# A fused attention and FFN kernel on one core: batch 0's scores as float32 products, and one decode form for all weight pieces

## The chip, the cores and the metric

The kernel runs on one core of one Trainium2 chip. The metric is the device time of one execution in microseconds (us). Three runs of the kernel before gave 784.2, 790.73 and 792.31 us; their median, 790.73 us, is the time before.

## What is computed

The reference is windowed attention followed by a two-layer FFN with a rational activation, in float32 (cut to what matters):

```
batch, n_heads, seq, head_dim = 4, 8, 768, 64      n_global, n_local = 8, 96
scores = (q @ k.T) / sqrt(D)
keep   = (key < n_global) | (0 <= rel < n_local)   # rel = query - key
scores += -2**-(h+1) * dist                        # head h's slope
a = softmax(where(keep, scores, -1e9));  o = a @ v # per head
x = o, heads side by side                          # (3072, 512)
h = x @ w_in                                       # w_in 512 x 2048
g = (a0 + a1 h + a2 h^2 + a3 h^3) / (1 + |b0||h| + |b1| h^2 + 1e-6)
out = g @ w_out                                    # w_out 2048 x 512
```

q, k, v and out are float32. The weights arrive as 64-bit numbers; the kernel reads each as two 32-bit words (`raw[:, :, 1]` and `raw[:, :, 0]`, `top` and `low` in `decode`) and builds a float32 number from them.

## The kernel before

**Units, chunks and steps.** Tokens are taken in 12 chunks of 256 (two tiles of 128). Attention is done in units: one unit `u` is one tile of 128 queries and one pair of heads, so there are 8 units in a chunk, 96 in all, and the first 24 units (`RAWQ = 24`) are batch 0. The FFN is done in items `f`, 8 for each chunk, each of 256 hidden columns. The main loop in `windowed()` runs over steps `t`; at step t it emits the load of unit t+4, the split of unit t+1, `st_qkT` and `st_qkE` of unit t, score and softmax of unit t-2, the transposes of unit t-3, the product with v of t-5, and FFN item f = t - 12 (`LAG`). So chunk 0's FFN items are steps 12 to 19.

**Order.** Each emitted piece carries a priority (1000 per step plus the table `PRI`, or `PRI_A` for the steps of the first FFN items). A planner that simulates the engines' time puts the instructions in order by these; on the chip each engine works its list in that order. Dependences are kept by semaphores. All DMAs are issued from SyncE's queue (SP), in one order as well.

**PSUM.** Four pools; the one that attention uses (`ps_t`, tag "t") has three buffers, shared by the transposed q and k (`tk`), the scores (`s`), the transposed probabilities (`tp`) and the attention output (`o`).

**Batch 0's scores.** For u < 24, `st_split` makes two float32r numbers out of each number of q and k: VectorE copies the rounded high part (line 377), GpSimd subtracts to get the low part (line 378). `st_qkT` transposes both parts of q and of k: 4 TensorE transposes (line 394). `st_qkE` brings them to SBUF on ScalarE: q with a scale for each head (line 412, twice), k (line 415) and, for a batch's first tile, the 8 global keys (line 417). High and low part of a head lie on the two halves of the 128 partitions, and two DMAs of 64 KB write the swapped copy of q that the second product needs (lines 413 and 414). `st_score` then takes 4 float32r products of 128 x 256 for each unit (line 450). From unit 24 on the split is done behind the transposes, by `raw_qkE` (lines 429 to 436), after a DMA within SBUF (line 372).

**Weight pieces.** `w_in` and `w_out` are decoded in 32 pieces of 128 x 512, in the order that `WSCHED` gives: 2 pieces at step 0, 4 at step 2, 6 each at 10 and 11, 4 at 12, 2 each at 13, 14 and 15, 4 at 18. Each piece is a load of 512 KB into one of three buffers (line 164, tile `r`), and then `decode` by one of four modes, listed in `MODE`:

- mode 0 (17 pieces): one ScalarE operation (line 172) and four VectorE operations: a maximum as a guard (174), a shift and mask (175), and two combinations of two tensors (177, 179);
- mode 1 (4 pieces): the same with the guard on GpSimd;
- mode 2 (9 pieces): one ScalarE operation (186), a conversion of 16 bits of the low word, here called the floor, on GpSimd (188), and two VectorE combinations (191, 193);
- mode 3 (2 pieces): the same with the floor on ScalarE (190).

**FFN.** Chunk 0's FFN uses the decoded float32 pieces as they are (lines 251 and 330). From chunk 1 on each product is made of three float32r products, of high and low parts (lines 259 and 335); for this `split_w` takes every piece apart at steps 15 to 26 (lines 210 and 211). Between the two products of an item stand `st_ew1` to `st_ew4` on ScalarE, VectorE and GpSimd (lines 283 to 315).

Of the kernel before, what the change touches and what calls it, by code (L numbers as in the profile page):

```python
# [17 lines left out]
P = 128  # L18
G = 8
# [5 lines left out]
RAW = 30  # L25
RAWQ = 24
LAG = 12
F2 = 2


# [4 lines left out]

SPLITS = {3: 0, 4: 1, 5: 6, 6: 7, 7: 10, 8: 19, 9: 20, 10: 25, 11: 26, 12: 28, 13: 29, 14: 32}

MODE = (3, 0, 2, 0, 2, 1, 2, 0, 0, 0, 0, 0, 0, 2, 2, 1, 0, 0, 0, 0, 0, 0, 0, 0, 2, 2, 1, 0, 3, 2, 1, 2)
HI_V = (2, 3, 6, 8, 11, 12, 13, 15, 16, 17, 18, 20, 21, 27, 28, 30, 31)
LO_V = (0, 2, 4, 5, 7, 8, 10, 13, 16, 17, 18, 20, 21, 22, 23, 24, 25)  # L40

# [55 lines left out]
def tile_kernel(ctx: ExitStack, tc: tile.TileContext, q, k, v, n_global, n_local,  # L97
# [24 lines left out]
    def unit(u):  # L122
        c, j = divmod(u, UPC)
        t, p = divmod(j, NPAIR)
        b, i = divmod(2 * c + t, NT)
        return c, t, p, b, i
# [32 lines left out]
    def decode(src, key):  # L159
        dst = full[key] = piece(F32, key)  # L160
        name = "r" + "_".join(map(str, key))
        raw = pl.ffn.tile([P, 2, 2, TOK], F32, tag="g", name=name, bufs=pl.gbufs)
        raw = raw.rearrange("p z a b -> p (z a b)").rearrange("p (f w) -> p f w", w=2)
        nc.sync.dma_start(out=raw.bitcast(I32), in_=src.rearrange("p (f w) -> p f w", w=2))
        bits = dst.bitcast(I32)
        top, low = raw.bitcast(I32)[:, :, 1], raw.bitcast(I32)[:, :, 0]
        half = raw.bitcast(U16).rearrange("p f (w z) -> p f w z", z=2)[:, :, 0, 1]
        mode = MODE[len(full) - 1]
        if mode < 2:


            nc.scalar.activation(out=dst, in_=raw[:, :, 1], func=AF.Abs)
            guard = nc.gpsimd if mode else nc.vector
            guard.tensor_scalar(out=dst, in0=dst, scalar1=1.125 * 2.0 ** -15, scalar2=None, op0=ALU.max)
            nc.vector.tensor_scalar(out=bits, in0=bits, scalar1=3, scalar2=0x3FFFFFFF,
                                    op0=ALU.logical_shift_left, op1=ALU.bitwise_and)
            nc.vector.scalar_tensor_tensor(out=bits, in0=top, scalar=-0x40000000, in1=bits,
                                           op0=ALU.bitwise_and, op1=ALU.bitwise_or)
            nc.vector.scalar_tensor_tensor(out=bits, in0=low, scalar=29, in1=bits,
                                           op0=ALU.logical_shift_right, op1=ALU.bitwise_or)  # L180
            return

        nc.scalar.activation(out=dst, in_=raw[:, :, 1], func=AF.Abs, scale=2.0 ** -112)
        if mode == 2:
            nc.gpsimd.tensor_scalar(out=low, in0=half, scalar1=2.0 ** -13, scalar2=FLOOR, op0=ALU.mult, op1=ALU.add)
        else:
            nc.scalar.activation(out=low, in_=half, func=AF.Copy, scale=2.0 ** -13, bias=FLOOR)  # L190
        nc.vector.scalar_tensor_tensor(out=low, in0=top, scalar=-0x80000000, in1=low,
                                       op0=ALU.bitwise_and, op1=ALU.bitwise_or)
        nc.vector.scalar_tensor_tensor(out=bits, in0=bits, scalar=3, in1=low,
                                       op0=ALU.logical_shift_left, op1=ALU.bitwise_or)
# [31 lines left out]
    def load_coef():  # L226
        nc.sync.dma_start(out=coef[:, 0:4], in_=ca.partition_broadcast(P))
        nc.sync.dma_start(out=coef[:, 4:6], in_=cb.partition_broadcast(P))
        nc.vector.memset(q1, 1.0 + 1e-6)
        nc.vector.memset(stats, 1e-9)  # L230

        rt = const.tile([P, 8], F32, name="rt")
        m, y, z, k = (rt[:, x:x + 1] for x in range(4))
        nc.scalar.activation(out=m, in_=coef[:, 5:6], func=AF.Abs)
        nc.vector.tensor_scalar(out=y, in0=m, scalar1=1e-36, scalar2=None, op0=ALU.max)
        nc.scalar.activation(out=y, in_=y, func=AF.Ln)
        nc.scalar.activation(out=y, in_=y, func=AF.Exp, scale=0.5)
        nc.vector.reciprocal(out=z, in_=y)
        nc.vector.scalar_tensor_tensor(out=z, in0=z, scalar=m, in1=y, op0=ALU.mult, op1=ALU.add)
        nc.vector.tensor_scalar(out=k, in0=m, scalar1=0.0, scalar2=0.5, op0=ALU.is_gt, op1=ALU.mult)  # L240
        nc.vector.tensor_tensor(out=b1, in0=z, in1=k, op=ALU.mult)
# [107 lines left out]

    kT = const.tile([P, H, 2, P], FR, name="kT")  # L350
    kG = const.tile([P, H, G], FR, name="kG")
    ident = const.tile([P, P], F32, name="ident")
    ident_r = const.tile([P, P], FR, name="ident_r")
    mask0 = const.tile([P, P], F32, name="mask0")
# [8 lines left out]
    def blocks_of(x, i):  # L363
        return x if i else x[..., 0, :]

    def st_split(u):
        p = unit(u)[2]
        if u >= RAWQ:

            if u % 2 == 0:  # L370
                s = pl.att.tile([P, 2, 4, D], FR, tag="rawq", name=f"sp{u}", bufs=2)
                nc.sync.dma_start(out=s.bitcast(F32), in_=nat[u // 2])
                sp[u] = sp[u + 1] = s
            return
        n = nat[u // 2][:, :, 2 * (p % 2):2 * (p % 2) + 2, :]
        s = pl.att.tile([P, 2, 2, 2, D], FR, tag="split", name=f"sp{u}", bufs=1)
        nc.vector.tensor_copy(out=s[:, :, :, 0, :], in_=n)
        nc.gpsimd.tensor_tensor(out=s[:, :, :, 1, :], in0=n, in1=s[:, :, :, 0, :], op=ALU.subtract)
        sp[u] = s

    def st_qkT(u):
        s = sp.pop(u)
        if u >= RAWQ:
            p = unit(u)[2]
            tk = pl.ps_t.tile([P, 2, P], FR, tag="t", name=f"tk{u}")
            for z in range(2):
                nc.tensor.transpose(out=tk[:, z, :], in_=s[:, z, 2 * (p % 2):2 * (p % 2) + 2].rearrange("p a d -> p (a d)"),  # L387
                                    identity=ident_r)
            tqk[u] = tk.bitcast(F32)
            return  # L390
        tk = pl.ps_t.tile([P, 2, 2, P], FR, tag="t", name=f"tk{u}")
        for z in range(2):
            for x in range(2):
                nc.tensor.transpose(out=tk[:, z, x, :], in_=s[:, z, x].rearrange("p a d -> p (a d)"),
                                    identity=ident_r)
        tqk[u] = tk

# [1 line left out]
    def st_qkE(u):  # L401
        c, t, p, b, i = unit(u)
        tk = tqk.pop(u)
        hs = slice(2 * p, 2 * p + 2)
        qT = pl.att.tile([P, 2, 2, P], FR, tag="qT", name=f"qT{u}")
        if u >= RAWQ:
            raw_qkE(p, i, tk, qT)
            qTs[u] = qT
            return
        for x in range(2):  # L410

            nc.scalar.activation(out=qT[:, 0, x], in_=tk[:, 0, x], func=AF.Copy, scale=float(2.0 ** (2 * p + x - 2)))
        nc.sync.dma_start(out=qT[0:D, 1].bitcast(F32), in_=qT[D:P, 0].bitcast(F32))
        nc.sync.dma_start(out=qT[D:P, 1].bitcast(F32), in_=qT[0:D, 0].bitcast(F32))
        nc.scalar.copy(out=kT[:, hs, i % 2, :], in_=tk[:, 1])
        if i == 0:
            nc.scalar.copy(out=kG[:, hs, :], in_=tk[:, 1, :, 0:G])
        qTs[u] = qT

# [20 lines left out]
    def st_score(u):  # L442
        c, t, p, b, i = unit(u)
        qT = qTs.pop(u)
        s_ps = pl.ps_t.tile([P, 2, 2, P], F32, tag="t", name=f"s{u}")
        for x in range(2):
            h = 2 * p + x
            rhs = kT[:, h] if i else kT[:, h, 0:1, :].broadcast_to([P, 2, P])
            for z in range(2):
                nc.tensor.matmul(out=s_ps[:, x], lhsT=qT[:, z, x, :], rhs=rhs, start=(z == 0), stop=(z == 1))  # L450
        if 1 <= i < NT - 1:
            nc.gpsimd.tensor_copy(out=kT[:, 2 * p:2 * p + 2, i % 2, 0:G], in_=kG[:, 2 * p:2 * p + 2, :])
        if i == 0:
            mk = mask0
        else:
            mk = masks[:, 0:2, :] if i % 2 else masks[:, 1:3, :]
        pr = pl.att.tile([P, 2, 2, P], F32, tag="prob", name=f"pr{u}")
        st = stats[:, u % 4]
        for x in range(2):
            h = 2 * p + x  # L460
            nc.vector.tensor_tensor_reduce(  # L461
                out=blocks_of(pr[:, x], i), in0=blocks_of(s_ps[:, x], i), in1=mk,
                scale=-(2.0 ** -(h + 1)), scalar=3e38, op0=ALU.add, op1=ALU.min, accum_out=st[:, x:x + 1])
        prob[u] = (pr, st)
# [83 lines left out]
    def windowed():  # L548
# [4 lines left out]
        make_identity(nc, ident)  # L553
        nc.vector.tensor_copy(out=ident_r, in_=ident)
        nc.vector.tensor_copy(out=nf, in_=ni)
        load_coef()
        st_split(0)
        st_split(1)

        nl, ng = nf[:, 0:1], nf[:, 2:3]  # L560
        scr = tmp("scr").rearrange("p a (b w) -> p (a b) w", w=P)
# [205 lines left out]
```

## Time and profile before

| | |
|---|---|
| runs | 784.2, 790.73, 792.31 us; median 790.73 |
| profiled execution | span 786.6 us (the page gives the span and no separate time around it) |
| TensorE busy | 735.9 us, 94% of the span |
| VectorE busy | 636.1 us, 81% |
| ScalarE busy | 588.3 us, 75% |
| GpSimd busy | 480.1 us, 61% |
| DMA | 86.38 MB, mean 110 GB/s |

The engines are named PE (TensorE), PEld (its weight loads), DVE (VectorE), ACT (ScalarE), POOL (GpSimd) and SP (SyncE) in the profile. A row of a table by stage gives for one stretch of time the busy microseconds of each engine with the number of instructions behind (x), then the granted TensorE clock as a share of full speed, the mean busy share of the DMA engines, and GB/s. A row of the table of waits says who waited for whom: microseconds in total, how often, and the longest. A row for one line of the code gives the shortest, median and longest duration in ns. A float32 product shows as two matmul records, a float32r product as one.

### The profile page before, as it was taken

To read this page: it belongs to the slowest core of one execution; us is meant where nothing else is said; L and a number is where in the kernel's file an instruction comes from. 1 tells how busy PE (TensorE), PEld (TensorE's weight loads), DVE (VectorE), ACT (ScalarE), POOL (GpSimd) and SP (SyncE) were. 2 spreads that over 40 slices of the span, in tenths; PEclk is the share of its full clock that TensorE was granted. 3 is DMA by queue.
4 is the path that set the end of the run, shared out by engine and by line. 5 is a ranking of instruction groups with operands and counts; after the bars stand their busy time and mean duration, and the time that the engine had idled before them with its cause. 6 is when DMAs were issued, how large, how long until landed. Compare 5 with 4: busy or idle time off the path is not lost.

```text
span 786.6 us, 16348 instructions
## 1 busy us (share of the span) xinstructions
PE 735.9 (94%) x5040; PEld 636.9 (81%) x5040; DVE 636.1 (81%) x1669; ACT 588.3 (75%) x1467; POOL 480.1 (61%) x512
## 2 busy tenths in 40 slices
PE   3678988899999999999999999999999999999995
PEld 2467646688898899898888898888898988988983
DVE  5888998989878887878778789788788688776664
ACT  4777675767888787787778787787887787776763
POOL 3867567977766655656556666656566656564350
PEclk9998999899999999999999999999999999999999
DMA  7785444413333353444443444454434433320000
GB/s 184 209 242 177 116 124 153 127 55 71 98 84 109 93 142 92 116 135 110 102 123 98 122 123 118 108 142 113 125 91 110 144 93 103 105 62 14 27 1 33
DMA packets 137856, 86.38 MB, mean 110 GB/s; under 512 B 85792, under 2 KB 118560, under 8 KB 137760
## 3 DMA queue, kind: packets, MB, share of 16 engines
q1 hardware_dynamic: 137760, 85.24, 39.0%
q8 instruction: 43, 0.70, 0.4%
q14 instruction: 53, 0.43, 0.2%
HBM read 35.92 MB, written 6.29 MB: 54 GB/s over the span
## 4 chain that ended last, share of the span: by engine, by line
PE 73%; DVE 9%; DMA 5%; ACT 5%; POOL 4%; issue 3%; SPq 0%; DVEq 0%; POOLq 0%; ACTq 0%
PE h L259 29%; PE acc L335 28%; PE s L450 5%; PE o L522 4%; PE tp L504 3%; POOL pr L483 2%; DMA r<-in_moe_w_in_dram 2%; PE acc L330 2%; PE h L251 1%; DMA r<-in_moe_w_out_dram 1%; PE tk L387 1%; ACT pr L471 1%; DVE pr L461 1%; DVE q L305 1%; DVE fu L290 1%
## 5 line engine op out<-in xcount | busy, mean ns | idle before, releaser
L335 PE MATMUL acc<-wout_h,g 128*128 128x512 f32 x704 | 242.0, 402 | 1.2 <-ACT g L314 1.1
L483 POOL TENSOR_SCALAR pr<-pr,stats 128x256 f32<-128x256 f32 (+1 forms) x192 | 178.5, 940 | 68.5 <-DVE stats L476 24.8
L259 PE MATMUL h<-xh,win_h 128*128 128x256 f32 x704 | 202.7, 288 | 3.3 <-DVE fu L291 3.3
L259 PE MATMUL h<-xl,win_h 128*128 128x256 f32 x704 | 199.2, 283 | 0.0
L292 POOL TENSOR_TENSOR fa<-fa,fs 128x512 f32<-128x512 f32 x95 | 124.2, 1307 | 107.6 <-ACT fs L285 101.1
L335 PEld LDWEIGHTS acc<-wout_h,g 128*128 128x128 f32 x704 | 126.6, 188 | 24.3 <-issue 3.3
L315 POOL TENSOR_TENSOR g<-fu,g 128x512 fp32r<-128x512 f32 x87 | 112.8, 1296 | 54.3 <-ACT g L314 41.2
L259 PEld LDWEIGHTS h<-xh,win_h 128*128 128x128 f32 x704 | 133.6, 190 | 10.4 <-DVE fu L291 5.2
L259 PEld LDWEIGHTS h<-xl,win_h 128*128 128x128 f32 x704 | 133.3, 189 | 3.9 <-issue 0.3
L283 ACT ACTIVATE fu<-h,coef 128x512 f32<-128x512 f32 (+1 forms) x97 | 75.1, 774 | 43.0 <-PE h L259 34.2
L471 ACT ACTIVATE pr<-pr,stats 128x256 f32<-128x256 f32 (+1 forms) x192 | 93.2, 490 | 14.6 <-DVE stats L461 13.7
L304 DVE SCALAR_TENSOR_TENSOR fu<-fu,coef,q 128x512 f32<-128x512 f32 (+1 forms) x97 | 71.7, 739 | 36.4 <-ACT q L300 35.3
L299 ACT ACTIVATE fs<-fa,coef 128x512 f32<-128x512 f32 (+1 forms) x97 | 69.8, 720 | 34.8 <-POOL fa L292 31.9
L290 DVE TENSOR_TENSOR fu<-fu,h 128x512 f32<-128x512 f32 (+1 forms) x97 | 65.6, 676 | 16.3 <-ACT fs L285 15.5
L450 PE MATMUL s<-kT,qT 128*128 128x256 f32 x384 | 73.1, 311 | 2.6 <-DMA qT<-qT 2.3
L291 DVE SCALAR_TENSOR_TENSOR fu<-fu,coef,h 128x512 f32<-128x512 f32 (+1 forms) x97 | 71.5, 737 | 1.2
L305 DVE SCALAR_TENSOR_TENSOR q<-fa,coef,q 128x512 f32<-128x512 f32 (+1 forms) x97 | 72.2, 744 | 0.0
L507 DVE COPY pT<-tp 128x512 f32<-128x512 f32 (+1 forms) x75 | 48.4, 645 | 29.4 <-PE tp L504 28.8
L461 DVE CUSTOM_DVE_ANT_0 pr<-s,masks 128x256 f32<-128x256 f32 x160 | 61.3, 419 | 10.3 <-PE s L450 6.7
L314 ACT CAST g<-fu 128x512 fp32r<-128x512 f32 (+1 forms) x89 | 54.8, 616 | 17.9 <-DVE fu L306 17.5
L306 DVE SCALAR_TENSOR_TENSOR fu<-q,fu 128x512 f32<-128x512 f32 (+1 forms) x97 | 66.1, 681 | 1.1
L285 ACT ACTIVATE fs<-h,coef 128x512 f32<-128x512 f32 (+1 forms) x97 | 66.4, 685 | 0.7
(280 smaller groups left out, 1633.3 us busy)
## 6 DMA issues: line engine op xcount, KB each, us to landing
raw<-pr SPq DMA_DIRECT2D x58, 256.0 KB
qT<-qT SPq DMA_DIRECT2D x192, 64.0 KB
sp<-nat SPq DMA_DIRECT2D x36, 256.0 KB
r<-in_moe_w_in_dram SPq DMA_DIRECT2D x16, 512.0 KB
r<-in_moe_w_out_dram SPq DMA_DIRECT2D x16, 512.0 KB
nat<-in_q_dram SPq DMA_DIRECT2D x48, 128.0 KB
nat<-in_k_dram SPq DMA_DIRECT2D x48, 128.0 KB
vt<-in_v_dram SPq DMA_DIRECT2D x48, 128.0 KB
```

The costliest lines, as they stand in the source:

```text
L259: nc.tensor.matmul(out=hps[f][:, y, :], lhsT=w[:, fs], rhs=x[:, ct, :], start=(n == 0), stop=(n == 3 * NCT - 1))
L283: nc.scalar.activation(out=u, in_=h, func=AF.Identity, scale=a3, bias=a2)
L290: nc.vector.tensor_tensor(out=u, in0=u, in1=h, op=ALU.mult)
L291: nc.vector.scalar_tensor_tensor(out=u, in0=u, scalar=a1, in1=h, op0=ALU.add, op1=ALU.mult)
L292: side(f).tensor_tensor(out=a, in0=a, in1=s, op=ALU.add)
L304: nc.vector.scalar_tensor_tensor(out=u, in0=u, scalar=a0, in1=r, op0=ALU.add, op1=ALU.mult)
L305: nc.vector.scalar_tensor_tensor(out=r, in0=a, scalar=q1, in1=r, op0=ALU.add, op1=ALU.mult)
L315: side(f).tensor_tensor(out=g[:, 1, ys], in0=u, in1=g[:, 0, ys], op=ALU.subtract)
L335: nc.tensor.matmul(out=acc, lhsT=gs[f][:, z, y, ts], rhs=w, start=(ft == 0 and n == 0), stop=(ft == NFT - 1 and n == 2))
L450: nc.tensor.matmul(out=s_ps[:, x], lhsT=qT[:, z, x, :], rhs=rhs, start=(z == 0), stop=(z == 1))
L471: nc.scalar.activation(out=d, in_=d, func=AF.Exp, scale=-1.0, bias=st[:, x:x + 1], accum_out=st[:, 2 + 2 * x:3 + 2 * x])
L483: nc.gpsimd.tensor_scalar(out=d, in0=d, scalar1=st[:, 6 + x:7 + x], scalar2=None, op0=ALU.mult)
```

## The change

Two things are changed. Batch 0's scores (u < 24) are made from q and k as they are: two float32 transposes, a copy of each head's q into its own half of a zeroed tile `qzero` (so that the 128 rows of one product hold one head's 64 numbers and 64 zeros), and two float32 products for each unit in place of four float32r ones; for a batch's first tile they are 128 columns wide in place of 256. `st_split` does nothing any more for u < 24, and the two DMAs that swapped q's halves are gone. And `decode` has one form: the one with two VectorE operations, its floor on ScalarE for the 12 pieces in `FLOOR_ACT` and on GpSimd for the other 20.

```diff
+QZ = 3
-MODE = (3, 0, 2, 0, 2, 1, 2, 0, 0, 0, 0, 0, 0, 2, 2, 1, 0, 0, 0, 0, 0, 0, 0, 0, 2, 2, 1, 0, 3, 2, 1, 2)
+FLOOR_ACT = (0, 3, 7, 9, 11, 15, 17, 19, 21, 23, 27, 28)
...
-        mode = MODE[len(full) - 1]
-        if mode < 2:
-            nc.scalar.activation(out=dst, in_=raw[:, :, 1], func=AF.Abs)
-            guard = nc.gpsimd if mode else nc.vector
-            guard.tensor_scalar(out=dst, in0=dst, scalar1=1.125 * 2.0 ** -15, scalar2=None, op0=ALU.max)
-            nc.vector.tensor_scalar(out=bits, in0=bits, scalar1=3, scalar2=0x3FFFFFFF,
-                                    op0=ALU.logical_shift_left, op1=ALU.bitwise_and)
-            nc.vector.scalar_tensor_tensor(out=bits, in0=top, scalar=-0x40000000, in1=bits,
-                                           op0=ALU.bitwise_and, op1=ALU.bitwise_or)
-            nc.vector.scalar_tensor_tensor(out=bits, in0=low, scalar=29, in1=bits,
-                                           op0=ALU.logical_shift_right, op1=ALU.bitwise_or)
-            return
         nc.scalar.activation(out=dst, in_=raw[:, :, 1], func=AF.Abs, scale=2.0 ** -112)
-        if mode == 2:
+        if len(full) - 1 in FLOOR_ACT:
+            nc.scalar.activation(out=low, in_=half, func=AF.Copy, scale=2.0 ** -13, bias=FLOOR)
+        else:
             nc.gpsimd.tensor_scalar(out=low, in0=half, scalar1=2.0 ** -13, scalar2=FLOOR, op0=ALU.mult, op1=ALU.add)
-        else:
-            nc.scalar.activation(out=low, in_=half, func=AF.Copy, scale=2.0 ** -13, bias=FLOOR)
...
+    k32 = const.tile([P, NPAIR, 2, P], F32, name="k32")
+    kG32 = const.tile([P, NPAIR, G], F32, name="kG32")
+    qzero = const.tile([P, QZ, 2, P], F32, name="qzero")
...  (st_split)
-        nc.vector.tensor_copy(out=s[:, :, :, 0, :], in_=n)
-        nc.gpsimd.tensor_tensor(out=s[:, :, :, 1, :], in0=n, in1=s[:, :, :, 0, :], op=ALU.subtract)
...  (st_qkT, u < RAWQ)
-        for z in range(2):
-            for x in range(2):
-                nc.tensor.transpose(out=tk[:, z, x, :], in_=s[:, z, x].rearrange("p a d -> p (a d)"),
-                                    identity=ident_r)
+            for z in range(2):
+                nc.tensor.transpose(out=tk[:, z, :], in_=n[:, z, 2 * (p % 2):2 * (p % 2) + 2].rearrange("p a d -> p (a d)"),
+                                    identity=ident)
...  (st_qkE, u < RAWQ)
-            nc.scalar.activation(out=qT[:, 0, x], in_=tk[:, 0, x], func=AF.Copy, scale=float(2.0 ** (2 * p + x - 2)))
-        nc.sync.dma_start(out=qT[0:D, 1].bitcast(F32), in_=qT[D:P, 0].bitcast(F32))
-        nc.sync.dma_start(out=qT[D:P, 1].bitcast(F32), in_=qT[0:D, 0].bitcast(F32))
-        nc.scalar.copy(out=kT[:, hs, i % 2, :], in_=tk[:, 1])
+            own = slice(x * D, (x + 1) * D)
+            nc.scalar.activation(out=qz[own, x], in_=tk[own, 0], func=AF.Copy, scale=float(2.0 ** (2 * p + x - 2)))
+        nc.scalar.copy(out=k32[:, p, i % 2, :], in_=tk[:, 1])
         if i == 0:
-            nc.scalar.copy(out=kG[:, hs, :], in_=tk[:, 1, :, 0:G])
+            nc.gpsimd.tensor_copy(out=kG32[:, p, :], in_=k32[:, p, 0, 0:G])
...  (st_score)
+            if u < RAWQ:
+                nc.tensor.matmul(out=blocks_of(s_ps[:, x], i), lhsT=qT[:, x, :], rhs=blocks_of(k32[:, p], i),
+                                 start=True, stop=True)
+                continue
...  (windowed)
+        for x in range(2):
+            nc.gpsimd.memset(qzero[(1 - x) * D:(2 - x) * D, :, x, :], 0.0)
-        st_split(0)
-        st_split(1)
```

More of the change, by code (lines that the diff above doesn't have):

```diff
@@ L366, in st_split, with st_qkT @@
     def st_split(u):
-        p = unit(u)[2]
[L368 to L376, printed above, removed]
-        nc.vector.tensor_copy(out=s[:, :, :, 0, :], in_=n)
[L378 to L384, printed above, removed]
+        if u >= RAWQ and u % 2 == 0:
+            s = pl.att.tile([P, 2, 4, D], FR, tag="rawq", name=f"sp{u}", bufs=2)
+            nc.sync.dma_start(out=s.bitcast(F32), in_=nat[u // 2])
+            sp[u] = sp[u + 1] = s
+    def st_qkT(u):
+        p = unit(u)[2]
+        if u < RAWQ:
+            tk = pl.ps_t.tile([P, 2, P], F32, tag="t", name=f"tk{u}")
+            n = nat[u // 2]
+            for z in range(2):
+                nc.tensor.transpose(out=tk[:, z, :], in_=n[:, z, 2 * (p % 2):2 * (p % 2) + 2].rearrange("p a d -> p (a d)"),
+                                    identity=ident)
+            tqk[u] = tk
+        else:
+            s = sp.pop(u)
             tk = pl.ps_t.tile([P, 2, P], FR, tag="t", name=f"tk{u}")
@@ L389, in st_qkT @@
             tqk[u] = tk.bitcast(F32)
-            return
-        tk = pl.ps_t.tile([P, 2, 2, P], FR, tag="t", name=f"tk{u}")
-        for z in range(2):
-            for x in range(2):
-                nc.tensor.transpose(out=tk[:, z, x, :], in_=s[:, z, x].rearrange("p a d -> p (a d)"),
-                                    identity=ident_r)
-        tqk[u] = tk
     def st_qkE(u):
@@ L403, in st_qkE @@
         tk = tqk.pop(u)
-        hs = slice(2 * p, 2 * p + 2)
-        qT = pl.att.tile([P, 2, 2, P], FR, tag="qT", name=f"qT{u}")
         if u >= RAWQ:
+            qT = pl.att.tile([P, 2, 2, P], FR, tag="qT", name=f"qT{u}")
             raw_qkE(p, i, tk, qT)
@@ L409, in st_qkE @@
             return
+        qz = qzero[:, u % QZ]
         for x in range(2):
-            nc.scalar.activation(out=qT[:, 0, x], in_=tk[:, 0, x], func=AF.Copy, scale=float(2.0 ** (2 * p + x - 2)))
-        nc.sync.dma_start(out=qT[0:D, 1].bitcast(F32), in_=qT[D:P, 0].bitcast(F32))
-        nc.sync.dma_start(out=qT[D:P, 1].bitcast(F32), in_=qT[0:D, 0].bitcast(F32))
-        nc.scalar.copy(out=kT[:, hs, i % 2, :], in_=tk[:, 1])
+            own = slice(x * D, (x + 1) * D)
+            nc.scalar.activation(out=qz[own, x], in_=tk[own, 0], func=AF.Copy, scale=float(2.0 ** (2 * p + x - 2)))
+        nc.scalar.copy(out=k32[:, p, i % 2, :], in_=tk[:, 1])
         if i == 0:
-            nc.scalar.copy(out=kG[:, hs, :], in_=tk[:, 1, :, 0:G])
-        qTs[u] = qT
+            nc.gpsimd.tensor_copy(out=kG32[:, p, :], in_=k32[:, p, 0, 0:G])
+        qTs[u] = qz
     def raw_qkE(p, i, tk, qT):
@@ L447, in st_score @@
             h = 2 * p + x
+            if u < RAWQ:
+                nc.tensor.matmul(out=blocks_of(s_ps[:, x], i), lhsT=qT[:, x, :], rhs=blocks_of(k32[:, p], i),
+                                 start=True, stop=True)
+                continue
             rhs = kT[:, h] if i else kT[:, h, 0:1, :].broadcast_to([P, 2, P])
@@ L450, in st_score @@
                 nc.tensor.matmul(out=s_ps[:, x], lhsT=qT[:, z, x, :], rhs=rhs, start=(z == 0), stop=(z == 1))
-        if 1 <= i < NT - 1:
+        if 1 <= i < NT - 1 and u < RAWQ:
+            nc.gpsimd.tensor_copy(out=k32[:, p, i % 2, 0:G], in_=kG32[:, p, :])
+        elif 1 <= i < NT - 1:
             nc.gpsimd.tensor_copy(out=kT[:, 2 * p:2 * p + 2, i % 2, 0:G], in_=kG[:, 2 * p:2 * p + 2, :])
```

## The prediction

> **What bounds the kernel now.** I read the page first, then a table by stages, then the waits within the early stages. From the page, the slices of the span:
>
> ```profile
> span 786.6 us, 16348 instructions
> PE   3678988899999999999999999999999999999995
> ...
> DVE  5888998989878887878778789788788688776664
> ...
> PEclk9998999899999999999999999999999999999999
> ```
>
> Each digit is a fortieth of the span, 19.7 us. TensorE is at 9 from the ninth digit on, and in the eight before it is not; there VectorE is mostly as full as TensorE or fuller. So there are two regimes, and the whole change (units 0 to 23, and pieces decoded from step 0 to 18) lies in the first. The stages in numbers, with cuts at 12 us (masks built, first scores read), 60 us (chunk 0's FFN under way) and 156 us (chunk 1's FFN begins):
>
> ```profile
> core 0: us, PE busy (x) PEld busy (x) DVE busy (x) ACT busy (x) POOL busy (x), PEclk, DMA share, GB/s
> 0.00:12.00 12.00, 2.68 (x14) 2.20 (x15) 4.07 (x27) 3.24 (x12) 3.37 (x12) 1.00 0.62 138
> 12.00:60.00 48.00, 31.35 (x170) 24.75 (x170) 41.63 (x132) 33.24 (x106) 34.61 (x41) 1.00 0.81 229
> 60.00:156.00 96.00, 83.85 (x432) 59.74 (x431) 90.92 (x199) 70.20 (x169) 67.12 (x64) 0.91 0.48 141
> 156.00:200.00 44.00, 42.60 (x289) 36.79 (x289) 38.63 (x93) 29.81 (x76) 33.74 (x34) 0.96 0.25 65
> 200.00:690.00 490.00, 488.57 (x3589) 438.36 (x3586) 400.17 (x1111) 392.44 (x995) 300.75 (x331) 1.00 0.41 112
> ```
>
> From 200 to 690 us TensorE is busy 488.57 of 490 us, and none of its work there is touched. What the early stages lose or gain is therefore passed on whole to the end. Between 60 and 156 us VectorE is busy 90.92 of 96 us (95%) against TensorE's 83.85 (87%, at a clock of 0.91): VectorE is the tighter of the two. Between 12 and 60 us VectorE has 41.63 of 48, and DMA is at 0.81. The waits up to 60 us, and then of 60 to 156 us:
>
> ```profile
> PE tk L394 <- POOL sp L378: 13.9, 6, 5.5
> ...
> PE tp L504 <- POOL pr L483: 5.9, 5, 2.5
> PE s L450 <- DMA qT<-qT: 2.3, 1, 2.3
> ```
>
> ```profile
> PE h L251 <- DVE fu L291: 3.3, 3, 1.9
> PE tp L504 <- POOL pr L483: 3.3, 1, 3.3
> PE acc L330 <- DVE w_10f L179: 2.2, 1, 2.2
> ```
>
> In the first list TensorE's largest wait, 13.9 us, is for the split that the change removes; in the second it waits for VectorE (the FFN's polynomial, a late piece) and for GpSimd's normalisation.
>
> **The change part by part. VectorE.** The copy of the split (L377), the guard (L174) and the shift (L175) go. Each by stage, 12 to 60 and 60 to 156 us:
>
> ```profile
> 12.00:60.00 48.00, 3.83 (x10) 1.00 0.81 229
> 60.00:156.00 96.00, 4.49 (x11) 0.91 0.48 141
> ...
> 12.00:60.00 48.00, 3.42 (x8) 1.49 (x1) 1.00 0.81 229
> 60.00:156.00 96.00, 5.13 (x9) 4.66 (x3) 0.91 0.48 141
> ...
> 12.00:60.00 48.00, 4.50 (x9) 1.00 0.81 229
> 60.00:156.00 96.00, 6.83 (x12) 0.91 0.48 141
> ```
>
> The order is L377, L174 (VectorE, then GpSimd), L175. VectorE loses 3.83 + 3.42 + 4.50 = 11.75 us in the first stage and 4.49 + 5.13 + 6.83 = 16.45 us in the second. The two combinations of a piece stay, under other line numbers, at the same price. VectorE is left with 41.63 - 11.75 = 29.9 of 48 us, and 90.92 - 16.45 = 74.5 of 96 us.
>
> **GpSimd and ScalarE.**
>
> ```profile
> 12.00:60.00 48.00, 8.63 (x10) 1.00 0.81 229
> 60.00:156.00 96.00, 8.54 (x10) 0.91 0.48 141
> ...
> L188 POOL TENSOR_SCALAR r<-r x9: 644/676/1100, 20.2 to 141.9; 128x512 int32<-128x512 uint16 x9
> ...
> L190 ACT ACTIVATE r<-r x2: 657/670/682, 15.3 to 128.8; 128x512 int32<-128x512 uint16 x2
> ...
> L415 ACT CAST kT<-tk x24: 346/380/422, 6.6 to 165.5; 128x256 fp32r<-128x256 f32 x24
> ...
> L430 ACT CAST kT<-tk x144: 243/248/265, 177.1 to 691.2; 64x128 fp32r<-64x128 f32 x144
> ```
>
> The first two rows are GpSimd's subtraction (L378). GpSimd loses it and four guards and gains 11 floors (20 against 9). Fourteen pieces were decoded by 60 us, so 5 of the 11 fall before and 6 behind. First stage: 34.61 - 8.63 - 1.49 + 5 x 0.68 = 27.9 us; second: 67.12 - 8.54 - 4.66 + 6 x 0.68 = 58.0 us. ScalarE gains 10 floors (12 against 2), 4 before 60 us and 6 behind, at 0.67 us; its copy of k becomes half as wide, and I take the 64 x 128 row's 0.25 us for 0.38: first stage 33.24 + 2.7 - 1.3 = 34.6 us, second 70.20 + 4.0 - 1.4 = 72.8 us. The scaled copies of q keep their number; bounds for one on half the partitions are no change and a tenth less, and I take no change. The floors add a wait for a piece's load to both engines: behind it stand on GpSimd the normalisation (L483), on ScalarE the exponentials and the FFN's reads of h, and TensorE waits for these. The few copies of global keys that go from ScalarE to GpSimd take 0.2 us each. Zeroing `qzero` is two memsets, bounded by nothing and some 1 us; GpSimd is idle then, waiting for the first load, and I take nothing. If it is late, unit 0's copy of q is late by that 1 us.
>
> **DMA and SP's queue.**
>
> ```profile
> L413 SPq DMA_DIRECT2D qT<-qT x24: 461/467/554, 6.7 to 165.6; - x24
> ...
> SPq L413 <- ACT kT L415: 23.7, 14, 4.8
> ...
> qT<-qT SPq DMA_DIRECT2D x20, 64.0 KB
> ```
>
> 48 issues of 0.47 us go, and with them a wait of 23.7 us in SP's queue up to 165 us, behind which the loads of pieces and of q, k and v stand. The 20 transfers between 12 and 60 us are 1.3 MB of the 11 MB that 229 GB/s move in 48 us: DMA falls from 0.81 x 48 = 39 to about 34 us.
>
> **TensorE.** This is what the change costs. From the chain that ended last, and then from the rows of four lines:
>
> ```profile
> 76.52 3.46 PE h L251 x16
> ...
> 159.88 3.43 PE acc L330 x8
> ...
> 190.17 2.83 PE h L259 x24
> ...
> L251 PE MATMUL h<-x,w_0f x32: 379/380/483, 51.1 to 63.8; 128*128 128x256 f32 x32
> ...
> L330 PE MATMUL acc<-w_0f,fu x4: 593/593/595, 80.8 to 83.0; 128*128 128x512 f32 x4
> ...
> L394 PE MATMUL tk<-ident_r,sp x96: 221/304/455, 5.5 to 163.8; 128*128 128x128 f32 x96
> ...
> L504 PE MATMUL tp<-ident,pr x104: 270/273/477, 18.5 to 235.2; 128*128 128x128 f32 x104
> ```
>
> A float32r product 256 wide takes 2.83 / 24 = 0.118 us in a stream; a float32 one is two records of 3.46 / 16 = 0.216 us, 0.432 us. A unit of 256 keys has 4 x 0.118 = 0.47 us now and 2 x 0.432 = 0.86 us then: +0.39 us, for 20 units 7.8 us; the 4 units of a first tile, half as wide, gain 0.04 each. Four float32r transposes (L394) become two float32 ones (as L504's with `ident`): by the medians 4 x 0.304 - 2 x 0.273 = 0.67 us less for each unit, by the extremes 2 x 0.477 - 4 x 0.221 = 0.07 us more; I take nothing, since they overlap in a stream. In all +7.7 us, of which 11 units, 4.3 us, lie between 60 and 156 us.
>
> **The sum, by stages.** Between 60 and 156 us the busiest engine is then TensorE with 83.85 + 4.3 = 88.1 us, VectorE and ScalarE having 74.5 and 72.8. I take 88 us for the stage: 8 us gained. The bounds are 0 (waits only change their names) and 16.5 (88.1 less the 8.6 us that a clock of 0.91 over 96 us costs). Between 12 and 60 us the busiest are then ScalarE at 34.6 and DMA at 34, against VectorE's 41.6 now; the same 48 / 41.6 on 34.6 gives 40 us, 8 us less. The chain has latencies that don't shrink in proportion, and TensorE's units grow by 3.5 us there, so I take 6; bounds 0 and 13.9, the wait for the split. Up to 12 us, the split's four operations leave the mask's path: 1 us, bounds 0 and 3. Behind 156 us two units add 0.8 us on a full TensorE, which I put into the roundings. Sum: 8 + 6 + 1 = 15 us, a span of 771.6. The page gives only the span; the median stands 790.73 - 786.6 = 4.1 us above it, so I forecast 790.73 - 15 = 775.7 us.
>
> **The rivals.**
>
> *The clock comes back as well.* The clock dips to half in pieces:
>
> ```profile
> 67.00:74.00 7.00, 6.02 (x14) 4.79 (x15) 6.84 (x17) 7.00 (x20) 4.56 (x4) 0.51 0.53 143
> ...
> 114.00:119.00 5.00, 4.66 (x10) 2.16 (x11) 5.00 (x14) 3.53 (x11) 3.40 (x4) 0.66 0.33 76
> ```
>
> Two of four such stretches. TensorE is short of work around them, waiting for L291 and for the late piece of L179. If denser work keeps the clock at 1.00, another 8.6 us go: 767 us. For it speaks that the operations removed are VectorE's, for which those waits were; against it that the chain from exponential to normalisation still leaves holes. The Trainium skill ("TensorE: Matmul & The Clock Gate", Part 1 and "HAM oscillation") says that a clock gate halves TensorE's clock after an idle window of about 3.4 us and opens again after a busy one. The dips agree in their two levels; whether the holes close, no row can say.
>
> *The gain is absorbed.* The chain of a unit, score to exponential to normalisation to transposes, passes through three PSUM buffers and four engines in order; 22 floors that wait for loads now stand in ScalarE's and GpSimd's lists ahead of L471 and L483. If these set the pace, VectorE only waits more: 783 to 791 us, 787 in the middle. TensorE's 5.9 and 3.3 us of waits for L483 speak for it; that GpSimd's load falls in both stages speaks against.
>
> *Slower: float32 scores on a full TensorE.* If TensorE's order already sets the pace of steps 12 to 23 and early units aren't quicker, its 7.7 us are added and nothing is returned: 798.4 us. It decides from the point where TensorE's busy share before 156 us is really work and not waiting. For it: 87% between 60 and 156 us. Against: a stream of the products there (4 pieces' columns x 32 records of L251 at 0.216 us; 16 pieces x 4 of L330 at 3.43 / 8 = 0.43) is 27.6 + 27.5 us, so a good part of the 83.85 is stretched by waits and the half clock.
>
> **How the numbers follow.** The forecast (769 to 783) has 0.45, the clock (757 to 769) 0.20, absorption (783 to 792) 0.22, slower (792 to 803) 0.13. The range of 760 to 792 leaves out the last and the lowest end of the second. A change under 1%, 7.9 us, can't be told from none here: the three runs lie 8 us apart. Under 782.8 us are 0.43 of the first case, the second and 0.02 of the third: 0.65 for faster. Over 798.6 us is about half of the last case, with an allowance for a planner that orders all engines anew: 0.08. Within 1%: 0.27.
>
> **What would show it.** Right: no wait of TensorE for a split, VectorE at about 75 busy us in the 85 to 90 us that chunk 0's FFN then takes, the first record of L251's successor before 47 us instead of 51, full TensorE from about 150 us, and the rest as long as now. Wrong: new waits of TensorE for L483 or L471, or of these for a floor, of more than 5 us; the long stage from 200 us on changed in length by more than 3 us, which would mean that the new order and not the work moved the time; or scores of more than 0.9 us a unit.

## The result and the profile after

The changed kernel takes 774.38 us (median of 4 runs, 773.73 to 775.89) against 787.47 us for the kernel before, run beside it (783.98 to 792.31): a ratio of 0.9838, 95% interval 0.9805 to 0.9871, that is 13.1 us less. The forecast was 775.7 us, 15 us less, with a range of 760 to 792. Three executions in the experiments below, 912.68 and 1801.47 us of one kernel and 1210.43 us of another, were slow ones and are left out of the ratios.

The page of the changed kernel, its slices of the span:

```profile
span 772.3 us, 16080 instructions
PE   3678999999999999999999999999999999999995
...
DVE  4879998888888778887788888787788788685654
...
PEclk9999999999999999999999999999999999999998
```

TensorE is at 9 from the fifth slice instead of the ninth. Yet VectorE, which lost work, is no emptier in slices 4 to 9. The table by stages, with the cuts that the prediction used (columns as there):

```profile
0.00:12.00 12.00, 4.54 (x16) 2.97 (x16) 3.34 (x27) 4.82 (x16) 3.12 (x16) 1.00 0.62 144
12.00:60.00 48.00, 30.10 (x167) 22.31 (x168) 36.41 (x117) 40.77 (x118) 30.31 (x40) 0.96 0.75 226
60.00:156.00 96.00, 92.00 (x479) 65.44 (x478) 89.56 (x183) 76.90 (x180) 69.68 (x67) 0.98 0.39 120
156.00:200.00 44.00, 44.00 (x313) 39.50 (x312) 36.07 (x101) 34.54 (x90) 28.07 (x32) 1.00 0.25 66
```

VectorE is busy 89.56 of the 96 us behind 60 us, where the prediction left it 74.5. Fixed times mislead here, because work moves past the cuts. Nor is the cut at 156 us where chunk 1's FFN begins, as the prediction has it: in the kernel before its first product (line 259) stands at 137.5 us, and h of item 8 is read at 143.0. So the same table is cut again where ScalarE begins to read h of FFN items 0, 8, 12 and 20 (lines 283 before, 266 after). First the kernel before, then the one after:

```profile
0.00:61.20 61.20, 35.22 (x188) 28.03 (x189) 46.90 (x160) 37.06 (x119) 39.18 (x54) 1.00 0.77 208
61.20:143.00 81.80, 73.05 (x378) 51.78 (x378) 77.22 (x172) 59.85 (x143) 52.92 (x53) 0.92 0.49 147
143.00:178.30 35.30, 31.90 (x186) 25.63 (x185) 31.25 (x60) 23.53 (x59) 29.57 (x25) 0.90 0.27 72
178.30:235.10 56.80, 55.40 (x403) 49.72 (x401) 47.70 (x140) 45.72 (x117) 40.56 (x45) 1.00 0.34 86
235.10:786.60 551.50, 540.31 (x3894) 481.78 (x3891) 433.07 (x1141) 422.14 (x1031) 317.91 (x338) 1.00 0.35 98
```

```profile
0.00:57.90 57.90, 32.54 (x172) 23.51 (x173) 38.59 (x140) 43.49 (x131) 32.16 (x53) 0.97 0.72 204
57.90:133.70 75.80, 71.99 (x338) 49.09 (x337) 72.41 (x144) 60.09 (x139) 52.69 (x52) 0.98 0.41 130
133.70:162.10 28.40, 28.21 (x194) 23.70 (x193) 23.38 (x56) 23.88 (x59) 24.36 (x22) 1.00 0.31 86
162.10:219.50 57.40, 57.40 (x411) 51.67 (x410) 46.99 (x129) 46.13 (x117) 33.76 (x40) 1.00 0.31 83
219.50:772.30 552.80, 541.58 (x3885) 480.77 (x3883) 430.33 (x1141) 421.21 (x1030) 316.38 (x336) 1.00 0.33 98
```

The span is 14.3 us shorter: 3.3 us are gained before the first item, 6.0 in chunk 0's items and 6.9 in items 8 to 11; behind item 12 1.9 us are given back. The gain in items 8 to 11 goes with another place of the subtractions that take the decoded pieces apart for the float32r products (VectorE, then GpSimd; line 211 before, 194 after). Cut in the same places:

```profile
61.20:143.00 81.80, 4.72 (x4) 3.30 (x3) 0.92 0.49 147
143.00:178.30 35.30, 9.62 (x9) 8.82 (x7) 0.90 0.27 72
178.30:235.10 56.80, 2.88 (x4) 7.71 (x6) 1.00 0.34 86
```

```profile
57.90:133.70 75.80, 6.83 (x8) 10.63 (x8) 0.98 0.41 130
133.70:162.10 28.40, 6.89 (x9) 9.54 (x8) 1.00 0.31 86
162.10:219.50 57.40, 0.00 (x0) 0.00 (x0) 1.00 0.31 83
```

Before, 7 of the 32 were begun ahead of item 8 and 10 ran behind item 12 (one that crosses a cut counts on both sides); after, 16 are begun ahead and none is left behind. The last combination of a piece begins at 155.5 us before and at 117.9 after, and this work, which needs the pieces, comes forward into VectorE's freed time. So VectorE is still full up to item 8 (72.41 of 75.8 us), and TensorE has next to no hole from item 8 to item 20. The waits of TensorE up to the first item, after:

```profile
PE tp L485 <- POOL pr L464: 11.4, 6, 6.5
PE o L503 <- ACT k L390: 4.7, 2, 3.0
PE tk L364 <- DMA nat<-in_q_dram: 3.3, 1, 3.3
PE tk L364 <- ACT k L390: 2.2, 1, 2.2
PE s L424 <- ACT k L390: 1.4, 2, 0.7
```

The 13.9 us of waiting for the split are gone; the wait for the normalisation has grown from 5.9 to 11.4 us, and ScalarE, busy 43.49 of 57.90 us, is waited for in its place. In all TensorE is idle 61.20 - 35.22 = 26.0 us up to the first item before and 57.90 - 32.54 = 25.4 after: other waits have taken the place of the one that went.

### The profile page after: what moved, and what is told of

Read it like the earlier page. It is cut to its first block, busy times and chain, and to the rows that moved or that the text cites. A ratio compares the mean times of both kernels' runs of the same rounds, so it can differ in the third digit from the quotient of the medians.

```text
span 772.3 us, 16080 instructions
## 1 busy us (share of the span) xinstructions
PE 731.7 (95%) x4992; PEld 628.7 (81%) x4992; DVE 611.7 (79%) x1608; ACT 594.8 (77%) x1472; POOL 459.3 (59%) x501
## 4 chain that ended last, share of the span: by engine, by line
PE 76%; DVE 11%; DMA 5%; issue 3%; ACT 2%; POOL 2%; SPq 1%; DVEq 0%; ACTq 0%; POOLq 0%
PE h L242 31%; PE acc L318 31%; PE o L503 5%; PE s L429 4%; PE tp L485 3%; DMA r<-in_moe_w_in_dram 2%; DVE r L174 2%; PE tk L371 1%; DVE pr L442 1%; DVE q L288 1%; PE s L424 1%; DMA raw<-pr 1%; DVE fu L287 1%; DMA out_dram<-o 1%; POOL pr L464 1%
## 5 line engine op out<-in xcount | busy, mean ns | idle before, releaser
L318 PE MATMUL acc<-wout_h,g 128*128 128x512 f32 x704 | 245.6, 405 | 0.4 <-POOL g L298 0.4
L464 POOL TENSOR_SCALAR pr<-pr,stats 128x256 f32<-128x256 f32 (+1 forms) x192 | 173.1, 912 | 88.0 <-DVE stats L457 37.7
L282 ACT ACTIVATE fs<-fa,coef 128x512 f32<-128x512 f32 (+1 forms) x97 | 69.5, 719 | 35.0 <-POOL fa L275 32.1
L442 DVE CUSTOM_DVE_ANT_0 pr<-s,masks 128x256 f32<-128x256 f32 x160 | 61.2, 418 | 9.8 <-PE s L429 6.0
L268 ACT ACTIVATE fs<-h,coef 128x512 f32<-128x512 f32 (+1 forms) x97 | 66.4, 684 | 0.8 <-DMA out_dram<-o 0.4
L267 ACT ACTIVATE fa<-h,coef 128x512 f32<-128x512 f32 (+1 forms) x97 | 65.6, 676 | 1.1 <-DMA out_dram<-o 1.0
```

The costliest lines, as they stand in the source:

```text
L282: nc.scalar.activation(out=s, in_=a, func=AF.Ln, bias=q1)
L318: nc.tensor.matmul(out=acc, lhsT=gs[f][:, z, y, ts], rhs=w, start=(ft == 0 and n == 0), stop=(ft == NFT - 1 and n == 2))
L442: nc.vector.tensor_tensor_reduce(out=blocks_of(pr[:, x], i), in0=blocks_of(s_ps[:, x], i), in1=mk, scale=-(2.0 ** -(h + 1)), scalar=3e38, ...
L464: nc.gpsimd.tensor_scalar(out=d, in0=d, scalar1=st[:, 6 + x:7 + x], scalar2=None, op0=ALU.mult)
```

## The experiments

Each was timed beside the kernel before, whose median stood between 787.3 and 788.2 us; ratios are to it. Differences to the kernel after are taken between ratios (1% is 7.9 us). The last columns, in us, are the lengths of the stages above, the time at which h of item 20 is read and the time from there to the end, each from one profiled execution. Those of decode alone, split unused and the second new deal of before took 784.0, 785.3 and 788.1 us, 2.5 to 3.7 under their medians; differences of that size between stages say little.

| kernel | median us | ratio, 95% interval | to item 0 | items 0-7 | items 8-11 | item 20 at | from item 20 |
|---|---|---|---|---|---|---|---|
| before | 787.5 | 1 | 61.2 | 81.8 | 35.3 | 235.1 | 551.5 |
| after | 774.38 | 0.9838 (0.9805 to 0.9871) | 57.9 | 75.8 | 28.4 | 219.5 | 552.8 |
| decode alone | 786.73 | 0.9990 (0.9965 to 1.0016) | 66.4 | 78.0 | 27.8 | 228.5 | 553.5 |
| scores alone | 791.37 | 1.0042 (1.0014 to 1.0071) | 61.9 | 83.7 | 30.0 | 232.5 | 556.5 |
| combination twice | 787.45 | 0.9989 (0.9966 to 1.0012) | 60.6 | 79.8 | 32.1 | 228.9 | 556.3 |
| products twice | 788.85 | 1.0011 (0.9984 to 1.0038) | 62.1 | 81.7 | 31.1 | 233.2 | 553.1 |
| floors shifted | 776.81 | 0.9861 (0.9839 to 0.9882) | 57.2 | 78.9 | 29.2 | 222.2 | 552.7 |
| floors elsewhere | 785.34 | 0.9969 (0.9952 to 0.9986) | 64.9 | 80.0 | 28.8 | 231.1 | 552.3 |
| split unused | 787.82 | 0.9997 (0.9978 to 1.0015) | 63.2 | 82.3 | 27.9 | 230.7 | 552.4 |
| q by DMA | 783.12 | 0.9944 (0.9925 to 0.9963) | 61.9 | 80.9 | 27.5 | 227.7 | 553.0 |
| before, modes dealt anew, 1 | 788.95 | 1.0017 (0.9993 to 1.0041) | 59.2 | 87.5 | 32.2 | 236.3 | 550.6 |
| before, modes dealt anew, 2 | 791.83 | 1.0064 (1.0040 to 1.0089) | 64.9 | 75.8 | 33.6 | 233.0 | 553.3 |
| after, floors dealt anew, 1 | 775.54 | 0.9857 (0.9825 to 0.9888) | 59.2 | 76.7 | 27.6 | 220.9 | 552.8 |
| after, floors dealt anew, 2 | 775.26 | 0.9852 (0.9822 to 0.9882) | 58.9 | 76.2 | 28.0 | 220.6 | 552.8 |

### One part alone

The theory was the prediction's: VectorE's load in the first 200 us set the time (V). Against it stood the shorter way from load to score (L) and the products added on TensorE (T).

```diff
 decode alone: the kernel before with FLOOR_ACT and the one decode form
 scores alone: the kernel after with MODE and the four decode forms
```

> The kernel before with the new decode form alone (batch 0's scores as before). Against the kernel before VectorE loses 8.6 + 11.3 = 19.9 busy us of guards and shifts. If VectorE's load in the first 200 us set the time (theory V), some half of it comes back: 10 us faster than before, ratio about 0.987, and the last combination of a piece ends near 125 us instead of 156.6. If the shorter way from load to score (no split, no transfer within SBUF, a freer SP queue) made the gain (theory L), this kernel gains 0 to 3 us.

> The kernel after with the old four decode modes (batch 0's scores as after). VectorE loses 9.2 us of copies, GpSimd 20.6 us of subtractions, TensorE gains 7.7 us. Theory V: 1 to 4 us faster than before, the pieces still ready as late as before (about 150 us). Theory L: 9 to 13 us faster. If TensorE's added products are on the path (theory T): 3 to 8 us slower.

Neither gave what V said: decode alone is not told apart from the kernel before, scores alone is 0.4% slower. The two parts add up to +0.3%, and together they give -1.6%. The stages tell more than the medians. Scores alone begins item 20 2.6 us before the kernel before does, and loses 5.0 us from there to the end, where none of the changed work lies; so its +0.4% can't be read as the price of the products. The stages of the decode alone up to item 12:

```profile
0.00:66.40 66.40, 39.85 (x196) 31.47 (x197) 44.02 (x149) 41.41 (x127) 44.32 (x60) 0.97 0.76 214
66.40:144.40 78.00, 70.00 (x356) 48.81 (x355) 74.75 (x156) 61.08 (x145) 56.11 (x59) 0.96 0.45 130
144.40:172.20 27.80, 27.80 (x207) 23.83 (x206) 24.71 (x59) 23.48 (x60) 25.09 (x23) 1.00 0.39 104
```

Items 8 to 11 take 27.8 us, as in the kernel after. Not all of that need be the decode's: scores alone takes 30.0 us there with the four old forms, and other deals of the kernel before (below) 32.2 and 33.6 us against 35.3. The first item comes 5.2 us later than before. GpSimd, which has the floors on top of the split's subtractions, is busy 44.32 us up to there against 39.18, and TensorE waits for it at two places:

```profile
PE tk L376 <- POOL sp L360: 9.5, 3, 5.4
PE tp L486 <- POOL pr L465: 9.3, 6, 3.4
```

Together these are 18.8 us, no more than the 13.9 + 5.9 us before, so they don't explain the delay. ScalarE's list around the first read of h accounts for 3.4 of the 5.2 us:

```profile
65.83 0.68 ACT L168 ACTIVATE w_2f<-r 128x512 f32<-128x512 f32 x1 [2.00 <-DMA r<-in_moe_w_in_dram]
66.41 0.78 ACT L265 ACTIVATE fu<-h,coef 128x512 f32<-128x512 f32 x1
```

Item 0's products end at 61.9 us (60.1 in the kernel before), but h is read 4.5 us behind them instead of 1.1: a piece whose load had not landed stands ahead of the read. That is a matter of the planned order as much as of the change; the new deals of the kernel before reach the first item at 59.2 and 64.9 us.

### One load put back

```diff
 combination twice (decode, after)
         nc.vector.scalar_tensor_tensor(out=low, in0=top, scalar=-0x80000000, in1=low, ...)
+        nc.vector.scalar_tensor_tensor(out=low, in0=top, scalar=-0x80000000, in1=low, ...)
 products twice (st_score, u < RAWQ, after)
+                for _ in range(2):
                     nc.tensor.matmul(out=blocks_of(s_ps[:, x], i), lhsT=qT[:, x, :], ..., start=True, stop=True)
```

> The kernel after with the first combination of each piece on VectorE done twice (the second changes nothing): 32 x 0.68 to 0.76 = 22 to 24 busy us put back on VectorE, nothing else. Theory V: half of it or more comes back, 9 to 14 us slower than after. Theory L or T: under 4 us.

> The kernel after with each float32 score product of batch 0 done twice into the same place: 20 x 0.86 + 4 x 0.43 = 18.9 us more on TensorE. If TensorE sets the pace of the early stages after the change (theory T), 12 to 19 us slower than after; if VectorE still does (theory V), 2 to 8 us, since most of it lies in TensorE's gaps. From this the price of the change's own 7.7 us follows in proportion.

Both gave nearly the whole gain back or more: +1.5% (12 us) for VectorE, +1.7% (14 us) for TensorE, of the 18.9 us put on it. For the doubled combination the two profiled spans differ by 12.9 us, of which 3.5 lie behind item 20 (556.3 us against 552.8), where nothing was added, and 9.4 before it. V's number was met, and so was T's; V's own 2 to 8 us for TensorE was wrong. The rows of the doubled line and of the products, up to 200 us (line, engine, operation, count, busy us and mean ns), of the two kernels in turn:

```profile
L176 DVE SCALAR_TENSOR_TENSOR r<-r 128x512 int32<-128x512 int32 x32 | 25.6, 807 | 0.1
L174 DVE SCALAR_TENSOR_TENSOR r<-r 128x512 int32<-128x512 int32 x32 | 22.1, 697 | 8.4 <-ACT r L171 4.6 <-POOL r L173 3.7
```

```profile
L425 PE MATMUL s<-k,qzero 128*128 128x256 f32 (+1 forms) x192 | 47.8, 394 | 2.4 <-DVE stats L456 1.7 <-ACT k L390 0.7
```

Now the removed operations, brought back without what hung on them:

```diff
 split unused (st_split, u < RAWQ, after): the two operations, into a tile that nothing reads
+            nc.vector.tensor_copy(out=s[:, :, :, 0, :], in_=n)
+            nc.gpsimd.tensor_tensor(out=s[:, :, :, 1, :], in0=n, in1=s[:, :, :, 0, :], op=ALU.subtract)
 q by DMA (st_qkE, u < RAWQ, after): ScalarE writes qw, a second tile
-            nc.scalar.activation(out=qz[own, x], ...)
+            nc.scalar.activation(out=qw[own, x], ...)
+            nc.sync.dma_start(out=qz[own, x], in_=qw[own, x])
```

> The kernel after with the split of q and k put back, its result not used: 9.2 busy us more on VectorE and 20.6 on GpSimd, while the way from load to score stays short. The doubled combination cost 13 us for some 23 us of VectorE. If load is what counts (theory V), 5 to 8 us slower than after; if it was the waiting for the split that held the early units (theory L), 0 to 3 us.

> The kernel after with the scaled q of batch 0 brought into its half of the zeroed tile by a transfer within SBUF: ScalarE writes a second tile, and 48 transfers of 32 KB copy it, so that the scores wait for SP's queue and the transfer again, as before; no engine's load changes. Theory L: 5 to 10 us slower than after, the first FFN item later by 3 us or more. Theory V: within 3 us of after.

The split's load costs 1.6% (12.5 us), more than V said, though nothing reads its result: the kernel is then as slow as before. The waiting, put back alone, costs 1.1% (8 us), as L said. What the split's load does up to the first item:

```profile
0.00:63.20 63.20, 36.35 (x173) 26.39 (x174) 46.53 (x156) 43.98 (x131) 47.07 (x69) 0.95 0.69 194
...
PE tp L491 <- POOL pr L470: 15.8, 5, 8.3
```

GpSimd is busy 47.07 us instead of 32.16, and TensorE's wait for the normalisation, which stands in the same list, grows from 11.4 to 15.8 us. The wait alone proves little: with no work added it is 15.6 us in the deal called floors elsewhere, below. The transfer shows as a wait of its own in the other kernel:

```profile
PE s L426 <- DMA qzero<-qw: 8.8, 3, 6.2
```

### Equal work in another order

So many small things costing the same 8 to 14 us called for another theory: that the kernel after has a lucky order (O). Dealing floors or modes to other pieces leaves each engine's work as it is, and the planner orders anew.

```diff
 floors shifted    FLOOR_ACT = (1, 4, 8, 10, 12, 16, 18, 20, 22, 24, 28, 29)
 floors elsewhere  FLOOR_ACT = (1, 2, 5, 6, 10, 13, 14, 18, 22, 25, 26, 30)
```

> The kernel after with the 12 floors on ScalarE taken from other pieces (each number plus one): the same work on every engine, but the planner orders everything anew. Decode alone gave 1.5 us and scores alone minus 3 us where both gave 13, so either two bounds stood in series and both had to go (theory S), or the kernel after has by chance a good order and the others a bad one (theory O). S: within 3 us of the kernel after, 1.3 to 2% faster than before. O: 5 to 14 us slower than after.

> The kernel after with 12 other pieces' floors on ScalarE (1, 2, 5, 6, 10, 13, 14, 18, 22, 25, 26, 30): a second draw of the order at equal work. Theory S: within 3 us of the kernel after. Theory O: 5 to 14 us slower, and not the same as the other draw.

One draw stayed within 1.8 us of the kernel after, the other lost 10 us (1.3%). This settled nothing, since the second also deals the early pieces differently (two of the four at step 2 have their floor on ScalarE). So two draws of each kernel were taken with the numbers kept within every step:

> The kernel before with the same four decode modes dealt anew to the pieces within each step (0 3 | 0 2 1 2 | 0 0 0 2 0 0 | 2 0 0 2 1 0 | ... | 0 1 | 2 3 2 1): equal work on each engine in each step, another planned order. Equal work in another order moved the kernel after by 2 and by 11 us. Theory W (the work removed is worth the 13 us): the draws of before lie 10 us or more above the draws of after, here 788 to 798 us. Theory O (the 13 us are mostly the one good order): the draws of before lie at 780 to 790 us, as those of after do.

> A second draw of the kernel before (3 0 | 1 2 0 2 | 0 0 2 0 0 0 | 1 0 0 2 0 2 | ... | 0 1 | 1 2 3 2), equal work in each step. W: 788 to 798 us. O: 780 to 790 us.

> The kernel after with the floors on ScalarE dealt anew within each step (1, 4, 6, 8, 10, 12, 14, 18, 20, 22, 26, 30), equal work in each step. W: 773 to 780 us. O: 780 to 787 us.

> A further draw of the kernel after (0, 5, 8, 10, 11, 13, 16, 18, 21, 23, 27, 31), equal work in each step. W: 773 to 780 us. O: 780 to 787 us.

The draws of before lie at 789.0 and 791.8 us, those of after at 775.5 and 775.3. The first of before fits O's range too; the two of after do not, nor does the second of before. So O falls, and the removed work is worth the difference, 13 to 17 us by any pair of these four. Even the draw that lost (0.9969) is faster than all three orders of the kernel before (1, 1.0017 and 1.0064). But one order in five of the kernel after lost 10 us with no work added, and every experiment that put a load back had one order only: that all four were slower by such bad luck is unlikely, yet the price of each is not settled by one order.

The draw that lost shows where an order can lose it. ScalarE's list in it and then in the kernel after, around the first read of h:

```profile
62.40 0.67 ACT L169 ACTIVATE w_2f<-r 128x512 f32<-128x512 f32 x1 [2.09 <-DMA r<-in_moe_w_in_dram]
63.72 0.68 ACT L169 ACTIVATE w_6f<-r 128x512 f32<-128x512 f32 x1 [0.64 <-DMA r<-in_moe_w_out_dram]
64.29 0.66 ACT L171 ACTIVATE r<-r 128x512 int32<-128x512 uint16 x1
64.85 0.76 ACT L266 ACTIVATE fu<-h,coef 128x512 f32<-128x512 f32 x1
```

```profile
57.39 0.62 ACT L193 CAST wout_h<-w_4f 128x512 fp32r<-128x512 f32 x1
57.90 0.79 ACT L266 ACTIVATE fu<-h,coef 128x512 f32<-128x512 f32 x1
```

In the slower order two pieces whose loads had not landed, and a floor, stand ahead of the first read of h, and ScalarE sits idle for 2.09 and 0.64 us before them. Item 0's products end at 60.3 us there and at 56.0 in the kernel after; h is read 4.6 us behind them instead of 1.9. So ScalarE's list explains 2.7 of the 7 us by which the first item is late; for the rest of the 10 us no single cause was shown.

## Why the prediction was right, and where not

**The bound.** That what the first 200 us gain is passed on whole was right: from item 20 to the end the kernels take 551.5 and 552.8 us, under the 3 us named. It isn't so for every kernel here: scores alone and the combination twice take 556.5 and 556.3 us for the same work. Other signs of being right came as named: no wait for a split, the first FFN product at 41.5 us (before 47 was forecast), and TensorE full from about 134 us.

**VectorE's term.** The sum took 11.75 and 16.45 us from VectorE and left it at 29.9 and 74.5. The operations are gone, but the step "VectorE is left with" failed: 36.41 and 89.56 us were measured between the same cuts, since later work came forward. To compare equal work, the cut at 156 us is better set at the product of chunk 1 that stood there, the first with `w_1l`, and the cut at 60 us at the first item's read. The product's rows (first and last start at the end), then the stages, each first before and then after:

```profile
L259 PE MATMUL h<-xh,w_1l x176: 277/282/681, 156.3 to 745.3; 128*128 128x256 f32 x176
L242 PE MATMUL h<-xh,w_1l x176: 277/281/387, 143.2 to 730.4; 128*128 128x256 f32 x176
```

```profile
61.20:156.20 95.00, 82.85 (x427) 58.86 (x427) 89.92 (x197) 69.83 (x169) 66.12 (x64) 0.91 0.48 142
57.90:143.20 85.30, 81.49 (x397) 56.02 (x396) 81.19 (x162) 68.16 (x156) 59.14 (x58) 0.98 0.40 125
```

VectorE loses 8.7 us there and not 16.45, because 5.2 us more of the taking apart fall in this stage and its 33 combinations take as long as the 37 before (29 us); it stays busy for 95% of the stage. The stage still is 9.7 us shorter, near the sum's 8; the term up to the first item, 1 + 6, was too large, with 3.3 us; and some 3 us more come behind this mark, up to item 12, of which 1.9 are given back, where the sum had "roundings". Other marks shift these shares: item 8's read of h comes only 9.4 us earlier, chunk 1's first product 13.9. So the total of 15 us is near the 13.1 measured, partly by luck: a term that was too large made up for ones that were too small. The time itself, 1.3 us off, owes more to luck: the median before fell by 3.3 us with its fourth run. The 4.1 us between span and time took the two from different executions; in those of the kernel after it is 1.8 to 1.9 us.

**ScalarE and GpSimd.** ScalarE was put at 34.6 us between 12 and 60 us; it has 40.77, since more pieces and item 0's reads of h fall there. GpSimd was put at 27.9 and 58.0 us; it has 30.31 and 69.68, the second more than the 67.12 before, again because of the taking apart. The prediction named an added wait for L483 of more than 5 us as a sign of error; the wait grew by 5.5 us. This is where the 6 us up to the first item went wrong: their upper bound was the 13.9 us of waiting for the split, but TensorE's idle time there fell only from 26.0 to 25.4 us.

**TensorE's term.** A unit's two products in the kernel after, from the order of time:

```profile
59.07 1.03 PE L424 MATMUL s<-k,qzero 128*128 128x256 f32 x4
59.94 0.38 PE L485 MATMUL tp<-ident,pr 128*128 128x128 f32 x2
```

Three steps of 0.216 us and the last record's 0.38 give that 1.03 us, and the next instruction begins 0.87 us behind the first, so the size of 0.86 us held. Taking the cost into the new busiest engine was right in kind: 18.9 us more cost 14 us in the one order tried, 0.7 us for each. An estimate from this for the change's own 7.7 us is some 5 or 6, if the price is the same for the first microseconds, which no run shows.

**Adding the parts.** The sum treated the parts as terms. By the medians they are not: alone they give -0.1% and +0.4%. The profiled executions soften this: up to item 20 decode alone is 6.6 us ahead of the kernel before, scores alone 2.6 and both together 15.6, so together they still gain more than the sum of 9.2 us, but by 6.4 us, where the medians make it 15. An account that fits, and that no experiment shows by itself, is that two bounds stood in series: with the split in place, TensorE waits for it up to the first item (9.5 us in decode alone); with the four old decode forms, VectorE holds chunk 0's items, as in the scores alone:

```profile
61.90:145.60 83.70, 73.76 (x335) 49.87 (x334) 79.57 (x171) 59.12 (x140) 51.66 (x47) 0.94 0.35 108
```

VectorE is busy 79.57 of 83.7 us there. The experiments that put back one load each point the same way: VectorE's, GpSimd's with VectorE's, TensorE's or the transfer's wait, each made the kernel 8 to 14 us slower in the one order tried. Which of the split's two operations does it (9.2 us on VectorE, 20.6 on GpSimd) was not taken apart.

**The rivals.** *The clock* came back in part: the losses by it are (1 - 0.92) x 81.8 + (1 - 0.90) x 35.3 = 10 us before and (1 - 0.97) x 57.9 + (1 - 0.98) x 75.8 = 3 us after. TensorE's busy time up to item 20 fell with it, from 195.6 to 190.1 us, and these two runs don't say how much of the gain is the clock's. But the clock alone doesn't tell a fast kernel from a slow one. The kernel with the combination twice, as slow as before, and the second new deal of after, as fast as after, have

```profile
60.60:140.40 79.80, 71.20 (x339) 48.85 (x338) 77.43 (x161) 64.02 (x148) 50.84 (x49) 0.98 0.45 133
...
0.00:58.90 58.90, 34.30 (x175) 26.09 (x176) 38.03 (x142) 44.39 (x133) 32.80 (x53) 0.91 0.72 207
```

and a clock of 1.00 in the other two of these three stages: 2 us lost by the clock in the slow one, 5 in the fast one. Over the whole execution floors shifted has a clock of 0.986, the kernel before 0.985, and their spans are 774.9 and 786.6 us. The Trainium skill ("TensorE: Matmul & The Clock Gate", "HAM oscillation") counts half of the time spent at the half clock as added to a kernel's time. The half clock agrees with this case's trace (0.51 in a stretch of the kernel before); the time lost so doesn't put these kernels in order. *Absorption* is what the median of the decode alone looks like (786.73 us, the middle of that rival was 787), and its first item was held by a load in ScalarE's list, much as the rival said. *Slower* looks like the scores alone (+0.4%, 3.3 us), but not by its reason: the loss lies behind item 20, and the second new deal of before is slower still (+0.6%).

## What to carry to other kernels

Cut stages by what is done (the first read of an item, the first product with a weight) and not by time, by more than one mark, and ask of each engine that is relieved which later work will move into the room: that is where the gain shows. A part that measures as nothing alone may still belong to a gain, so parts are tried together as well as alone, and a part's loss is first looked for in the stages that it changes. And where a planner orders engines anew, deal equal work in another way a few times before a difference of 1% is put down to the work: here draws of one kernel lay up to 10 us apart.

## What was not expected of the hardware

The times of these kernels did not follow the granted clock (0.90 to 1.00 in the stages shown up to item 12). And the doubled combination on VectorE, the same instruction done twice over, took 697 ns in the mean at its first place and 807 ns at its second, 665 ns at the least in both; what holds the second up was not tried.
